# Keys and queries of batches 3 to 7 loaded by tokens and turned by DMA transposes, in a kernel for attention with beacons and an ELU layer

## The chip, the cores and the metric

The kernel runs on one core of one Trainium2 chip. The metric is the device time of one execution in microseconds (us); lower is better. A core has TensorE (PE, matrix products and transposes through a product with the identity), VectorE (DVE), ScalarE (ACT), GpSimd (POOL) and SyncE (SP), which here issues nearly all DMAs. TensorE writes to PSUM, from which VectorE or ScalarE copy. Each engine works through its own list of instructions in order, and waits on semaphores for the others.

## The reference

B = 8 batches, H = 8 heads, S = 576 tokens, 16 beacons for each batch and head, D = 64. Keys and values get the beacons ahead of the tokens; a token sees all beacons and the tokens up to itself. The attention's output, 4608 rows of 512, goes through two matrix products with an ELU between them (512 to 2048 to 512).

```python
    k_all = np.concatenate([beacon_k, k], axis=2)
    v_all = np.concatenate([beacon_v, v], axis=2)
    scores = scale * np.matmul(q, k_all.transpose(0, 1, 3, 2))
    causal[:, Nb:] = np.triu(np.ones((S, S), dtype=bool), k=1)
    scores = np.where(causal, -1000000000.0, scores)
    a = np.exp(scores - scores.max(-1, keepdims=True))
    a /= a.sum(-1, keepdims=True) + 1e-09
    attn_out = np.matmul(a, v_all)
    x = attn_out.transpose(0, 2, 1, 3).reshape(B * S, H * D)
    h = x @ w_in
    g = np.where(h > 0.0, h, np.exp(np.minimum(h, 0.0)) - 1.0)
    out = g @ w_out
```

All inputs lie in DRAM in fp32, and so does the output; the kernel computes with bf16 (scores) and fp16 (the rest).

## The kernel before

**The order.** The kernel is not written as loops. Each step is an `Op` with an engine, a key (its due time), an estimated duration, the steps that it depends on, and the buffer slots that it takes and gives back. `Plan.run` (L38) plays these through on a clock of its own: on each engine it starts the ready step with the lowest key whose slots are free, and then calls the steps' functions in the order found. So every engine's order of instructions, SP's too, comes from the keys and the estimated durations; the chip then runs each engine's list in order with semaphores. The steps of the pseudo-engine `DMA` stand for transfers; they issue nothing and only say when data are taken to have landed. One line of them is served by key, one after the other. `load` (L244) makes a step on SP and the transfer behind it, and L709 to L712 chain all loads in order of their keys. `place(b, a)` (L503) gives the key of batch b: 32 for each batch, 8 for each pair of heads, plus `SHIFT[b]`; `AT`, `AT0`, `PACES`, `W_AFTER`, `FIRST`, `LAG` and `URGE` (L490 to L501) are the other constants of the keys, and `ON_POOL` and `Q_ON_ACT` choose engines.

**Attention.** A unit of work is a pair of heads of one batch, n = 4 b + hp (32 pairs).

- `load_pair` (L263, DMA at L269): two DMAs load a pair's keys and queries, 288 KB each. A partition gets 9 neighbouring tokens of a head, so a run in DRAM is 9 x 64 fp32 values, 2304 B; keys lie on the even partitions, queries on the odd ones. `load_bk` (L255) and `cast_bk` (L260) bring a batch's beacon keys.
- `cast_pair` (L272): one instruction casts the pair to bf16 (tile `st`, 1152 values on each partition), on GpSimd for most pairs.
- `do_T` (L307; matmuls at L311 and L313): nine transposes of 128 x 128 on TensorE and one for the beacons, into a PSUM tile `tr` that shares its two slots (`sc`) with the scores. Batch 0 uses `do_T2` and `do_copy2` in place of `do_T`, `do_kT` and `do_qT`.
- `do_kT` (L343: two copies, L345 and L346) on VectorE and `do_qT` (L348: L351 on ScalarE or L353 on VectorE) copy `tr` into the bf16 tiles kT and qT, in order of tokens. There are `NKQ` = 4 such pairs of tiles.
- `do_SC` (L355): scores, keys on the partitions; `do_exp` (L368) exponentials on ScalarE into `et`; `do_mask` (L375) the causal mask on GpSimd.
- `load_v` (L285, DMA at L292) brings values by tokens, in 5 chunks of up to 128 tokens for each batch: a partition gets one token of all 8 heads, in runs of 64 fp32 values, 256 B. `cast_v` (L294) casts them on VectorE.
- `do_AV` (L383) multiplies with the values; a column of ones gives the sums. `do_norm` (L404: L411, L412) divides on VectorE into x16.
- x16 must be turned for the next product. Batches 0 and 1 do it on TensorE (`do_xT`, `do_xcopy`). From batch `XB` = 2 on `turn_x` (L280, L282) does it with five DMA transposes for a batch, issued by SP; each takes up to 128 rows of 512 fp16 values to 4 blocks of 128 partitions of `xT`.

**The ELU layer.** The 4608 rows are cut in 10 tiles (256, 256, then 512 rows). `do_mm1` (L444) makes a step of the hidden layer in PSUM (`hps`), `do_e` (L453) its exponential on ScalarE, `do_clamp` (L457) bounds it on GpSimd, `do_join` (L461) joins both on VectorE into `gt`; `do_mm2` (L471) multiplies with w_out into `ops`, `do_osb` (L480) copies on VectorE and `do_store` (L484) stores through SP. The weights come in four pieces each of w_in and w_out (512 KB each in fp16, 1 MB in DRAM), loaded and cast by DMAs that GpSimd issues (`load_w`, L298; `plan_w`, L545). Which step they come behind is `W_AFTER`: an index into `marks`, the sorted masks and beacon casts of the first batches.

PSUM's slots: `sc` 2, `ff` 4. Buffers in SBUF: `st` (fp32 pairs) 4, `sb` (bf16 pairs) 2, `vst` (fp32 values) 5, `gt` 20, `osb` 3.

Of the kernel before, what the change touches and what calls it, by code (L numbers as in the profile page):

```python
# [18 lines left out]
class Op:  # L19
    def __init__(self, eng, key, dur, fn, deps=(), take=(), give=(), mode=None, lat=0.03):  # L20
        self.eng, self.key, self.dur, self.fn = eng, key, dur, fn
        self.deps, self.take, self.give = [d for d in deps if d is not None], take, give
        self.mode, self.lat = mode, lat
        self.left, self.after = 0, []


class Plan:
# [10 lines left out]
    def run(self):  # L38
# [10 lines left out]
        mode = None  # L49
        for op in self.ops:  # L50
            if not op.left:
                heapq.heappush(ready[op.eng], (op.key, op.seq))
        events, order, now, n_left, tick = [], [], 0.0, len(self.ops), 0
        while n_left:
            for eng in ready:
                if free[eng] > now + 1e-9:
                    continue
# [36 lines left out]
            while events and events[0][0] <= now + 1e-9:  # L94
# [6 lines left out]
                for o in op.after:  # L101
                    o.left -= 1
                    if not o.left:
                        heapq.heappush(ready[o.eng], (o.key, o.seq))
# [8 lines left out]
def kernel(  # L113
# [86 lines left out]
    NG, NET, NKQ = 20, 8, 4  # L200
# [22 lines left out]
    kTs = [big.tile([P, SKP], BF16, name=f"kT_{i}") for i in range(NKQ)]  # L223
    qTs = [big.tile([P, S], BF16, name=f"qT_{i}") for i in range(NKQ)]
# [5 lines left out]
    with tc.tile_pool(name="psum", bufs=1, space=bass.MemoryType.PSUM) as psum:  # L230
# [4 lines left out]
            "st": 4, "sb": 2, "bk": 1, "vst": 5,  # L235
# [8 lines left out]
        def load(key, dur, fn, deps=(), take=(), issue=0.47):  # L244

            issue = add("SP", key, issue, fn, deps=deps, take=take)
            issues.append(issue)
            return add("DMA", key, dur, None, deps=[issue], lat=2.0)
# [6 lines left out]
        def load_bk(b):  # L255
            t = bks[b] = stage.tile([P, DM], FP32, tag="bk", name="bk32", bufs=1)
# [22 lines left out]

        def turn_x(b, blk):  # L280
# [4 lines left out]
        def load_v(b, jc):  # L285
            vst = vsts[b, jc] = stage.tile([P, H, D], FP32, tag="vst", name="vst", bufs=5)
# [197 lines left out]
        def do_store(tt, t4):  # L484
# [5 lines left out]
        SHIFT = [18.19, -1.67, -5.21, 9.28, 2.92, -5.56, -3.02, 18.21]  # L490
        AT = [-2.75, -0.54, -0.93, -0.06, 0.2, 1.01, 1.99, -16.61]
        AT0 = [[-45.78, -33.15, -38.79, -34.41], [-45.52, -23.75, -37.77, -41.96], [-33.6, -16.81, -31.44, -41.61]]
        PACES = [(-10.52, 1.48, 24.15, -2.31), (-10.42, 4.31, 27.52, 4.6), (37.71, 0.81, 11.65, 4.01), (83.94, 2.16, 31.7, 1.22), (112.53, 2.24, 29.18, 2.45)]
        W_AFTER = [[21.51, 12.09, 17.39, 6.76], [7.67, 24.47, 24.74, 25.24]]
        ON_POOL = "20010220"
        X_ON_ACT = "00"
        LAG = 17.55
        URGE = 72.32
        Q_ON_ACT = "01111110"
        FIRST = (  # L500
            "q2 k1 q1 v2 v1 k2 k3 q3 q5 v0 q4 k4 k5 v4 b1 v3 k6 q6 v6 v5 v9 q7 k7 v8 v7 ").split()  # L501
# [240 lines left out]
```

## Time and profile before

| | |
|---|---|
| median of 3 runs | 368.67 us (368.13 to 369.1) |
| the profiled execution's own time | 367.97 us |
| its span, from the first to the last instruction | 366.2 us |
| granted TensorE clock, mean | 0.989 |
| transposes of keys and queries on TensorE, L311 and L313, batches 1 to 7 | 280 matmuls in 28 groups |
| casts of pairs on GpSimd, L278 | 25, mean 1149 ns |
| copies to kT on VectorE, L345 and L346 | 28 each, mean 754 and 155 ns |
| copies to qT on ScalarE, L351 | 24, mean 649 ns |
| DMA transposes of x on SP, L282 | 30, median 1250 ns of issue, 2.5 us to landing |
| loads of keys and queries, L269 | 64, median 0.61 us of issue, 4.2 and 4.5 us to landing |
| loads of v, full chunks | 24, 5.3 us to landing |
| DMA queue of SP, share of 16 engines' span | 43.4% |
| DMA queue of GpSimd (weights) | 7.0% |

How to read it: the span lacks what lies around the first and last instruction. Busy time of an engine is the time in which one of its instructions ran; instructions of TensorE overlap each other. A row of 40 digits gives the busy share of 40 equal slices of the span, in tenths. The view of waits says which instruction waited for which other, for how long in total, how many times, and the longest. The DMA share of a stage is the mean over the core's 16 DMA engines of the time that packets took; two queues at work together can take it over 1.

### The profile page before, as it was taken

The page shows a single profiled execution, that of the slowest core. Times are in us where ns is not written, and L with a number is a line of the kernel's source. Part 1 is how long each engine was busy: PE and PEld are TensorE (multiplying, and loading weights), DVE is VectorE, ACT ScalarE, POOL GpSimd, SP SyncE. Part 2 cuts the span into 40 slices and gives each one's busy share as a digit, 9 for nine tenths or more (in the row PEclk, how much of TensorE's full clock was granted, in tenths as well). Part 3 has the DMA queues.
Part 4 walks back from the last instruction along what each step waited for, and adds up shares of the span by engine and source line. Part 5 has one row for each costly group of instructions (what it writes and reads, how often), then busy time and mean ns, then how long its engine had stood idle before and what let it go on. Part 6 is the DMA issues. An engine that isn't in the chain of part 4 may idle for free.

```text
span 366.2 us, 8353 instructions
## 1 busy us (share of the span) xinstructions
PE 346.9 (95%) x3240; PEld 191.7 (52%) x3240; DVE 213.3 (58%) x454; ACT 205.3 (56%) x308; POOL 190.6 (52%) x363
## 2 busy tenths in 40 slices
PE   1796999999999999999999999999999999999995
PEld 1564775755465556555555554544555544444442
DVE  1575367778864777765756765555666554554321
ACT  3775683568857786767677666435546534333100
POOL 3383582658855866757466656335534434344200
PEclk9998799999999999999999999999999999999999
DMA  7999995788137966957696600220000221000022
GB/s 215 295 235 243 235 164 148 179 233 285 55 68 203 273 83 161 208 146 197 143 235 170 135 30 29 57 68 29 31 29 30 57 68 57 30 29 29 30 94 78
DMA packets 73256, 46.54 MB, mean 127 GB/s; under 512 B 56321, under 2 KB 60417, under 8 KB 73217
## 3 DMA queue, kind: packets, MB, share of 16 engines
q1 hardware_dynamic: 68848, 41.53, 43.4%
q0 software_dynamic: 4224, 4.19, 7.0%
q8 instruction: 25, 0.41, 0.5%
q10 hardware_dynamic: 144, 0.29, 0.2%
q14 instruction: 15, 0.11, 0.1%
HBM read 37.22 MB, written 9.44 MB: 127 GB/s over the span
## 4 chain that ended last, share of the span: by engine, by line
PE 86%; DMA 5%; DVE 2%; POOL 2%; ACT 2%; SPq 1%; issue 1%; ACTq 0%; DVEq 0%
PE ops L476 34%; PE hps L449 33%; PE sc L362 7%; PE av L396 7%; PE tr L311 3%; DMA w_in<-in_moe_w_in_dram 3%; DMA st<-in_q_dram 1%; POOL et L377 1%; PE tr L321 1%; DMA vst<-in_v_dram 1%; ACT et L371 1%; DVE kT L345 1%; DVE gt L468 1%; SPq L282 0%; DVE v L296 0%
## 5 line engine op out<-in xcount | busy, mean ns | idle before, releaser
L449 PE MATMUL hps<-xT,w_in 128*128 128x512 f16 (+1 forms) x640 | 146.0, 363 | 2.8 <-DMA w_in<-in_moe_w_in_dram 2.2
L476 PE MATMUL ops<-w_out,gt 128*128 128x512 f16 x576 | 144.2, 379 | 0.0
L468 DVE SCALAR_TENSOR_TENSOR gt<-e,hps 128x512 f16<-128x512 f32 x144 | 97.6, 684 | 79.5 <-POOL e L459 79.3
L459 POOL TENSOR_SCALAR e<-e 128x512 f32<-128x512 f32 x144 | 89.5, 624 | 104.3 <-ACT e L455 101.5
L455 ACT ACTIVATE e<-hps 128x512 f32<-128x512 f32 x144 | 85.5, 599 | 90.8 <-PE hps L449 86.9
L371 ACT ACTIVATE et<-sc 128x800 f16<-128x800 f32 (+3 forms) x128 | 103.9, 864 | 22.0 <-PE sc L362 18.8
L449 PEld LDWEIGHTS <-w_in 128*128 128x128 f16 x640 | 60.5, 99 | 59.3 <-DMA w_in<-in_moe_w_in_dram 2.3
L476 PEld LDWEIGHTS <-gt 128*128 128x128 f16 x576 | 52.4, 98 | 57.5 <-issue 3.0
L377 POOL TENSOR_SCALAR_AFFINE_SELECT et<-et 128x256 f16<-128x256 f16 (+2 forms) x160 | 60.0, 402 | 40.4 <-ACT et L371 37.3
L396 PEld LDWEIGHTS <-et 128*128 128x128 f16 (+1 forms) x960 | 37.3, 100 | 10.8 <-issue 1.9
L396 PE MATMUL av<-v,et 128*128 128x65 f16 (+1 forms) x960 | 41.5, 197 | 0.6 <-POOL et L377 0.6
L362 PE MATMUL sc<-qT,kT 64*128 64x80 bf16 (+3 forms) x704 | 37.2, 238 | 3.4 <-ACT et L371 1.8
L482 DVE COPY osb<-ops 128x512 f32<-128x512 f32 x36 | 24.8, 689 | 23.8 <-PE ops L476 23.6
L362 PEld LDWEIGHTS <-kT 64*128 64x128 bf16 x704 | 21.8, 97 | 25.4 <-issue 19.2
L412 DVE TENSOR_TENSOR x<-av,rl 128x256 f16<-128x256 f32 (+2 forms) x68 | 32.0, 471 | 2.3
L278 POOL CAST st<-st 128x1152 bf16<-128x1152 f32 x25 | 28.7, 1149 | 8.1 <-PE tr L313 6.4
L351 ACT ACTIVATE qT<-tr 128x576 bf16<-128x576 bf16 x24 | 15.6, 649 | 19.8 <-DVE kT L346 12.0
L345 DVE COPY kT<-tr 128x576 bf16<-128x576 bf16 x28 | 21.1, 754 | 8.1 <-PE tr L313 7.7
L411 DVE RECIPROCAL rl<-av 128x4 f32<-128x4 f32 (+2 forms) x68 | 12.5, 183 | 16.6 <-PE av L396 15.5
L296 DVE CAST v<-vst 128x512 f16<-128x512 f32 (+1 forms) x40 | 18.9, 489 | 4.3 <-DMA vst<-in_v_dram 4.3
L311 PEld LDWEIGHTS <-st 128*128 128x128 bf16 x252 | 16.1, 98 | 5.6 <-issue 0.4
L311 PE MATMUL tr<-identb,st 128*128 128x128 bf16 x252 | 18.6, 219 | 0.1
(32 smaller groups left out, 69.0 us busy)
## 6 DMA issues: line engine op xcount, KB each, us to landing
st<-in_k_dram SPq DMA_DIRECT2D x32, 288.0 KB, 4.2
out_dram<-osb SPq DMA_DIRECT2D x36, 256.0 KB, 2.1
st<-in_q_dram SPq DMA_DIRECT2D x31, 288.0 KB, 4.5
vst<-in_v_dram SPq DMA_DIRECT2D x24, 256.0 KB, 5.3
w_in<-in_moe_w_in_dram POOLq DMA_DIRECT2D x4, 512.0 KB, 9.0
w_out<-in_moe_w_out_dram POOLq DMA_DIRECT2D x4, 512.0 KB, 8.4
vst<-in_v_dram SPq DMA_DIRECT2D x8, 224.0 KB, 4.0
vst<-in_v_dram SPq DMA_DIRECT2D x8, 160.0 KB, 5.0
```

Source lines behind the costliest of these rows:

```text
L278: eng.tensor_copy(out=dst, in_=src)
L311: nc.tensor.transpose(out=tr[:, P * g:P * g + P], in_=b16s[n][:, g].rearrange("p h d -> p (h d)"), identity=identb)
L362: nc.tensor.matmul(out=sc[:, h, o:o + w], lhsT=kT[D * h:D * h + D, P * jc:P * jc + P], rhs=qT[D * h:D * h + D, q0:q0 + w], start=True, sto ...
L371: nc.scalar.activation(out=et[:, :, 0:w], in_=scs[n, u][:, :, 0:w], func=AFT.Exp, bias=0.0, scale=float(1.0 / (D ** 0.5)))
L377: nc.gpsimd.affine_select(out=et[:, :, c0:c0 + dw], in_=et[:, :, c0:c0 + dw], compare_op=ALU.is_ge, fill=fill0, base=q0 + NB - P * jc, pat ...
L396: nc.tensor.matmul(out=av[:, c:c + D + 1], lhsT=ets[n, CUT.unit_of[jc, at]][0:m, h, col:col + P], rhs=v16[0:m, jc, 2 * hp + h, 0:D + 1], s ...
L412: nc.vector.tensor_tensor(out=x16s[b % 2][:, blks[0]:blks[0] + nb, P * hp:P * hp + P].rearrange("q i (h d) -> q i h d", d=D), in0=av[:, :, ...
L449: nc.tensor.matmul(out=hps[:, (hi - lo) * j:(hi - lo) * (j + 1)], lhsT=w_in16[:, cc, P * fc:P * fc + P], rhs=xT[cc][:, lo:hi], start=(cc = ...
L455: nc.scalar.activation(out=e, in_=hpss[tt, i], func=AFT.Exp, bias=0.0, scale=1.0)
L459: nc.gpsimd.tensor_scalar(out=e, in0=e, scalar1=1.0, scalar2=0.0, op0=ALU.min, op1=ALU.max)
L468: nc.vector.scalar_tensor_tensor(out=gt, in0=es[tt, i], scalar=1.0, in1=hpss[tt, i], op0=ALU.subtract, op1=ALU.max)
L476: nc.tensor.matmul(out=ops, lhsT=gts[tt, fc][:, P * t4:P * (t4 + 1)], rhs=w_out16[:, fc, :], start=(fc == 0), stop=(fc == NFC - 1))
```

## The change

From batch `PE_B` = 3 on, keys and queries take another way.

- They are loaded as v is (`load_tok`): for each batch 5 chunks of keys and 5 of queries, each up to 128 tokens of all 8 heads, in runs of 256 B. Beacon keys are the first 16 rows of the first key chunk, with a DMA of their own. Two chunks share an fp32 buffer.
- They are cast in 6 instructions for each batch (`cast_tok`): two chunks at once (1024 values on each partition), the fifth alone (512 values). The string `TOK` says which are on GpSimd ("1") and which on VectorE ("0").
- Each chunk is turned by one DMA transpose from SP (`turn_tok`) straight into kT or qT, 10 for each batch. It waits for the cast and for the scores of the batch two before.
- kT and qT are now two tiles for all four pairs of a batch (`kTa`, `qTa`), used by batches in turn: `NKQ` goes from 4 to 8 pairs. `gt` goes from 20 to 18 buffers, `vst` from 5 to 4, and beacon keys of the first batches use a `vst` buffer.
- The first scores of a batch from 3 on wait for all ten of its DMA transposes (`ready = turned[b]`). For these batches no transposes on TensorE and no copies to kT and qT are made, and no beacon casts.

Besides, the planner's picture of DMA changes: transfers are served in the order in which they were issued, on two lines (SP's and that of the weights) that take turns; at most 9 loads of SP are let into its line at once (`dq`); a piece of weights is four transfers. In the program itself the queues stay as they were: SP's for all but the weights (and one first load), GpSimd's for the weights. All constants of the keys were set anew, so the order of steps differs in all batches, with other engines for some casts of the first two batches (`ON_POOL`), copies to qT of batches 1 and 2 on VectorE (`Q_ON_ACT`), and other marks for the weights.

```diff
--- before.py
+++ after.py
...
 class Op:
-    def __init__(self, eng, key, dur, fn, deps=(), take=(), give=(), mode=None, lat=0.03):
+    def __init__(self, eng, key, dur, fn, deps=(), take=(), give=(), mode=None, lat=0.03, queue=0):
         self.eng, self.key, self.dur, self.fn = eng, key, dur, fn
         self.deps, self.take, self.give = [d for d in deps if d is not None], take, give
-        self.mode, self.lat = mode, lat
+        self.mode, self.lat, self.queue = mode, lat, queue
...
         free = dict.fromkeys(pending, 0.0)
-        mode = None
+        mode, lines, turn = None, ([], []), 0
+        def arrive(o):
+            if o.eng == "DMA":
+                lines[o.queue].append(o)
+            else:
+                heapq.heappush(ready[o.eng], (o.key, o.seq))
         for op in self.ops:
             if not op.left:
-                heapq.heappush(ready[op.eng], (op.key, op.seq))
+                arrive(op)
...
                 if free[eng] > now + 1e-9:
+                    continue
+                if eng == "DMA":
+                    if lines[0] or lines[1]:
+                        turn = 1 - turn if lines[1 - turn] else turn
+                        op = lines[turn].pop(0)
+                        free[eng] = now + op.dur
+                        heapq.heappush(events, (free[eng], tick, None))
+                        heapq.heappush(events, (free[eng] + op.lat, tick + 1, op))
+                        tick += 2
...
                 while first[eng] < len(line) and line[first[eng]][1] in done:
...
                     if not o.left:
-                        heapq.heappush(ready[o.eng], (o.key, o.seq))
+                        arrive(o)
...
         for _, _, op in order:
...
-    NG, NET, NKQ = 20, 8, 4
+    NG, NET, NKQ = 18, 8, 2 * HP
+    PE_B = 3
...
     stage = ctx.enter_context(tc.tile_pool(name="stage", bufs=2))
...
     x16s = [big.tile([P, NKC, DM], FP16, name=f"x16_{i}") for i in range(2)]
-    kTs = [big.tile([P, SKP], BF16, name=f"kT_{i}") for i in range(NKQ)]
-    qTs = [big.tile([P, S], BF16, name=f"qT_{i}") for i in range(NKQ)]
+    kTa = [big.tile([P, HP, SKP], BF16, name=f"kT_{i}") for i in range(2)]
+    qTa = [big.tile([P, HP, S], BF16, name=f"qT_{i}") for i in range(2)]
+    kTs = [t[:, hp] for t in kTa for hp in range(HP)]
+    qTs = [t[:, hp] for t in qTa for hp in range(HP)]
...
     bk16s = [big.tile([P, DM], BF16, name=f"bk16_{i}") for i in range(2)]
...
             "sc": 2, "ff": 4, "av": 2, "ops": 1, "et": NET, "rl": 2, "e": NE, "gt": NG, "osb": 3,
-            "st": 4, "sb": 2, "bk": 1, "vst": 5,
+            "st": 4, "sb": 2, "dq": 9, "vst": 4,
...
         add = plan.add
...
-            issue = add("SP", key, issue, fn, deps=deps, take=take)
+            issue = add("SP", key, issue, fn, deps=deps, take=take + ["dq"])
             issues.append(issue)
-            return add("DMA", key, dur, None, deps=[issue], lat=2.0)
+            return add("DMA", key, dur, None, deps=[issue], lat=2.0, give=["dq"])
...
         add("SP", -1e6, 0.8, None)
...
         def load_bk(b):
-            t = bks[b] = stage.tile([P, DM], FP32, tag="bk", name="bk32", bufs=1)
+            t = bks[b] = stage.tile([P, H, D], FP32, tag="vst", name="bk32", bufs=4).rearrange("p h d -> p (h d)")
...
+        def rows_of(is_k, c):
+            if not is_k:
+                return 0, min(P, S - P * c), P * c
+            r0 = NB if c == 0 else 0
+            return r0, kc_sz[c] - r0, P * c - NB + r0
+        def load_tok(b, is_k, c):
+            if (b, is_k, c // 2) not in f32s:
+                f32s[b, is_k, c // 2] = stage.tile([P, 2, G * D], FP32, tag="st", name="st32", bufs=4)
+            t = f32s[b, is_k, c // 2].rearrange("p h f -> p (h f)")[:, DM * (c % 2):DM * (c % 2) + DM]
+            t = t.rearrange("p (h d) -> p h d", h=H)
+            r0, n, lo = rows_of(is_k, c)
+            if is_k and c == 0:
+                nc.sync.dma_start(out=t[0:NB], in_=beacon_k[b].rearrange("h n d -> n h d"))
+            nc.sync.dma_start(out=t[r0:r0 + n], in_=(k if is_k else q)[b, :, lo:lo + n, :].rearrange("h s d -> s h d"))
+        def cast_tok(b, is_k, c, m, eng):
+            o = b16s[b, is_k, c // 2] = stage.tile([P, G, 2, D], BF16, tag="sb", name="st16", bufs=2)
+            r0, n, _ = rows_of(is_k, c + m - 1)
+            n = n if m == 1 else P
+            eng.tensor_copy(
+                out=o.rearrange("p g h d -> p (g h d)")[0:n, 0:DM * m],
+                in_=f32s[b, is_k, c // 2].rearrange("p h f -> p (h f)")[0:n, 0:DM * m])
+        def turn_tok(b, is_k, c):
+            r0, n, lo = rows_of(is_k, c)
+            t = (kTa if is_k else qTa)[b % 2]
+            nc.sync.dma_start_transpose(
+                out=t[:, :, P * c:P * c + r0 + n],
+                in_=b16s[b, is_k, c // 2].rearrange("p g h d -> p (g h d)")[0:r0 + n, DM * (c % 2):DM * (c % 2) + DM])
...
         def load_v(b, jc):
-            vst = vsts[b, jc] = stage.tile([P, H, D], FP32, tag="vst", name="vst", bufs=5)
+            vst = vsts[b, jc] = stage.tile([P, H, D], FP32, tag="vst", name="vst", bufs=4)
...
             r0 = NB if jc == 0 else 0
...
-        SHIFT = [18.19, -1.67, -5.21, 9.28, 2.92, -5.56, -3.02, 18.21]
-        AT = [-2.75, -0.54, -0.93, -0.06, 0.2, 1.01, 1.99, -16.61]
-        AT0 = [[-45.78, -33.15, -38.79, -34.41], [-45.52, -23.75, -37.77, -41.96], [-33.6, -16.81, -31.44, -41.61]]
-        PACES = [(-10.52, 1.48, 24.15, -2.31), (-10.42, 4.31, 27.52, 4.6), (37.71, 0.81, 11.65, 4.01), (83.94, 2.16, 31.7, 1.22), (112.53, 2.24, 29.18, 2.45)]
-        W_AFTER = [[21.51, 12.09, 17.39, 6.76], [7.67, 24.47, 24.74, 25.24]]
-        ON_POOL = "20010220"
+        SHIFT = [-1.59, -8.11, -4.8, -3.41, 4.52, 5.53, 8.01, 5.8]
+        AT = [-10.75, -2.37, -0.67, -1.23, -0.1, 1.04, 1.11, -20.16]
+        AT0 = [[-58.54, -53.13, -35.03, -42.4], [-45.14, -42.0, -36.41, -38.19], [-5.63, -27.76, -50.44, -20.85]]
+        PACES = [(-8.99, 2.27, 22.92, 3.9), (-2.72, 2.83, 27.52, 4.24), (38.17, 0.5, 9.24, 2.86), (79.65, 1.96, 26.14, 0.79), (105.01, 2.1, 30.59, 2.17)]
+        W_AFTER = [[7.88, -52.99, -9.09, 6.95], [16.42, 25.9, 20.56, 31.58]]
+        DMA_AT = [-127.66, -67.18, 46.75]
+        TOK = ("111001", "010110", "101011", "011001", "000000")
+        ON_POOL = "01202200"
         X_ON_ACT = "00"
-        LAG = 17.55
-        URGE = 72.32
-        Q_ON_ACT = "01111110"
+        LAG = 13.62
+        URGE = 62.52
+        Q_ON_ACT = "00011111"
         FIRST = (
-            "q2 k1 q1 v2 v1 k2 k3 q3 q5 v0 q4 k4 k5 v4 b1 v3 k6 q6 v6 v5 v9 q7 k7 v8 v7 ").split()
+            "v1 q1 k2 k1 k4 v0 q3 k3 v3 q2 v2 v4 q6 b1 q4 k7 q5 k5 v7 q7 v8 k6 v5 v6 v9 ").split()
...
             return 32 * (b - 1) + 8 * a + SHIFT[b]
...
             if hp == 0:
-                got = load(load_key(f"b{b}", place(b, 0) - 31), 0.2, partial(load_bk, b), take=["bk"])
+                got = load(load_key(f"b{b}", place(b, 0) - 31), 0.2, partial(load_bk, b), take=["vst"])
                 bk_in[b] = add("POOL", place(b, -0.9), 0.6, partial(cast_bk, b),
-                               deps=[got] + last_T.get(b - 2, []), give=["bk"])
+                               deps=[got] + last_T.get(b - 2, []), give=["vst"])
...
             gots = []
...
             got = add("POOL", after.key + 0.01, 0.8, partial(load_w, which, f4), deps=[after])
-            got = add("DMA", f4 - 300, 3.2, None, deps=[got], lat=2.5)
+            for _ in range(4):
+                got = add("DMA", 0, 0.8, None, deps=[got], lat=2.0 if _ == 3 else 0.0, queue=1)
             w_at.update({(which, 4 * f4 + c): got for c in range(4)})
+        turned, last_SC = {}, {}
+        def plan_tok(b):
+            turned[b] = []
+            for is_k in (True, False):
+                for c in range(0, NKC, 2):
+                    m = min(2, NKC - c)
+                    i = (0 if is_k else 0.5) + c // 2
+                    gots = [load(place(b, 0) - 30 + i + 0.01 * j, 1.2, partial(load_tok, b, is_k, c + j),
+                                 take=["st"] if j == 0 else [], issue=1.1 if is_k and c + j == 0 else 0.6) for j in range(m)]
+                    on_dve = TOK[b - PE_B][3 * (not is_k) + c // 2] == "0"
+                    cast = add("DVE" if on_dve else "POOL", place(b, DMA_AT[0]) + i, 0.36 * m if on_dve else 0.53 * m,
+                               partial(cast_tok, b, is_k, c, m, nc.vector if on_dve else nc.gpsimd),
+                               deps=gots, take=["sb"], give=["st"])
+                    for j in range(m):
+                        s = add("SP", place(b, DMA_AT[1]) + i, 1.25, partial(turn_tok, b, is_k, c + j),
+                                deps=[cast] + last_SC.get(b - 2, []))
+                        turned[b].append(add("DMA", place(b, DMA_AT[1]) + i, 0.6, None, deps=[s],
+                                             give=["sb"] if j == m - 1 else [], lat=1.9))
...
             b, hp = divmod(n, HP)
...
             key = AT0[0][hp] - 4 if b == 0 else at(AT[1])
-            ready = plan_T2(n, key) if b == 0 else plan_T(n, key)
+            ready = plan_T2(n, key) if b == 0 else plan_T(n, key) if b < PE_B else turned[b]
...
             steps = [((0,), AT0[0][hp]), ((1, 2), AT0[1][hp]), ((3,), AT0[2][hp])] if b == 0 else \
...
                 last_kq[n] = SC
+                last_SC.setdefault(b, []).append(SC)
...
                     w = CUT.width[u]
...
                             s = add("SP", at(AT[7]), 1.25, partial(turn_x, b, blk), deps=part.pop(blk))
-                            done = add("DMA", at(AT[7]), 0.5, None, deps=[s], lat=2.2)
+                            done = add("DMA", at(AT[7]), 0.6, None, deps=[s], lat=1.9)
...
                                 if lo <= BLOCKS[blk][0] < hi:
...
-        for t in kTs:
-            nc.vector.memset(t[:, SK:SKP], 0.0)
+        for t in kTa:
+            nc.vector.memset(t[:, :, SK:SKP], 0.0)
...
             plan_v(b)
+            if b >= PE_B:
+                plan_tok(b)
             for hp in range(HP):
-                plan_loads(b * HP + hp)
+                if b < PE_B:
+                    plan_loads(b * HP + hp)
...
```

## The prediction

> **What bounds the kernel now.** I read the shares of the engines first, then the same span in 40 slices, then who waited for whom on TensorE, and last the chain of waits in the middle of the span.
>
> ```profile
> span 366.2 us, 8353 instructions
> ...
> PE 346.9 (95%) x3240; PEld 191.7 (52%) x3240; DVE 213.3 (58%) x454; ACT 205.3 (56%) x308; POOL 190.6 (52%) x363
> ...
> PE   1796999999999999999999999999999999999995
> ...
> DMA  7999995788137966957696600220000221000022
> ```
>
> TensorE is busy 346.9 of 366.2 us, no other engine above 58%, and the row of slices puts TensorE's gaps in the first five slices and the last. The view of TensorE's waits from 50 us to the end has one entry:
>
> ```profile
> PE sc L362 <- ACT qT L351: 0.5, 1, 0.5
> ```
>
> So from 50 to 361 us nothing but TensorE's own work sets the time, and a TensorE instruction removed there shortens the kernel by its slot, as long as the other engines, the sync queue (SP) and the DMA engines keep up. The 19.3 us of gaps are 14.6 us in the first 50 us (start of loads, first pairs, the first weights) and the last copy and store.
>
> **What a removed transpose group is worth.** For batches 3 to 7, 20 pairs of heads lose their group of ten transposes. The chain of waits around one such group, in columns of start, length and what ran:
>
> ```profile
> 144.46 0.86 PE hps L449 x4
> 145.32 0.50 PE tr L311 x9
> 145.82 0.06 PE tr L313
> 145.88 0.18 PE av L396 x6
> ```
>
> From the first transpose to the next piece it is 145.88 - 145.32 = 0.56 us. The table of stages, restricted to that tile, gives the same group more:
>
> ```profile
> 200.00:210.00 10.00, 0.72 (x10) 0.82 (x2) 0.65 (x1) 1.00 0.69 170
> ```
>
> 0.72 us is the time from the first start to the modelled end of the last, and its last 0.16 us lie under the work behind. The start-to-start slot is what TensorE gets back: 20 x 0.56 = 11.2 us; the upper bound is 20 x 0.72 = 14.4 us. I take 11.2. The Trainium skill (Trainium Kernel Development and Optimization, Performance Expectations) says that matmul busy time is a bad measure because matmuls are pipelined. By that rule the 0.72 is not to be used, by the busy row alone the time would be 3.2 us lower; the trace agrees with the rule, 0.56 against 0.72.
>
> **What goes and comes on the other engines.** VectorE loses the copies to kT (754 + 155 ns, 20 times, 18.2 us) and batch 7's to qT (4 x 746 ns, 3.0); ScalarE loses 16 copies to qT (649 ns, 10.4 us); GpSimd loses 20 casts of pairs (1149 ns, 23.0) and 5 of the beacons (600 ns, 3.0). The casts by tokens come in: by the string TOK VectorE gets 12 of 1024 elements and 4 of 512, GpSimd 8 and 6. Scaled from the casts of 1152 elements (750 ns on VectorE, 1149 on GpSimd), that is 12 x 0.67 + 4 x 0.35 = 9.4 us and 8 x 1.02 + 6 x 0.55 = 11.5 us. So from batch 3 on VectorE has 11.8, ScalarE 10.4 and GpSimd 14.5 us less to do. Against that the new string for qT moves the copies of batches 1 and 2 from ScalarE to VectorE, 8 x 0.75 = 6 us in a stage (57 to 97 us) where VectorE is busy 31.0 of 40. All of this lies under TensorE, at a cost of nothing; without the cover a late copy costs the score step behind it.
>
> **The DMA engines.** This is what the change pays with. The tables of stages (length, busy time of PE, PEld, DVE, ACT and POOL, granted clock, DMA share, GB/s):
>
> ```profile
> 97.00:103.00 6.00, 6.00 (x74) 3.36 (x72) 4.38 (x10) 5.30 (x9) 4.67 (x9) 1.00 0.32 101
> 103.00:110.00 7.00, 7.00 (x82) 4.03 (x81) 4.08 (x10) 3.31 (x5) 3.68 (x7) 1.00 0.38 74
> ...
> 300.00:309.00 9.00, 9.00 (x44) 4.09 (x42) 4.68 (x8) 3.58 (x6) 3.58 (x6) 1.00 0.08 30
> ...
> 57.00:97.00 40.00, 39.88 (x489) 24.03 (x488) 31.03 (x73) 26.20 (x39) 25.40 (x47) 1.00 0.69 194
> 103.00:163.00 60.00, 59.49 (x666) 33.34 (x664) 39.45 (x86) 41.65 (x62) 39.98 (x74) 1.00 0.72 172
> 163.00:213.50 50.50, 50.50 (x551) 28.29 (x550) 32.52 (x73) 35.41 (x52) 30.89 (x60) 1.00 0.68 160
> ```
>
> Share times length is busy time of all 16 engines; sync's timeline tells what was issued. 97 to 103 holds two loads by pairs: 1.92 us, 0.96 each. 103 to 110 holds five DMA transposes of x and next to nothing else: 2.66, 0.53 each. 300 to 309 holds one store, 0.72. From 57 to 97 there are 14 loads by pairs, 4 stores and 10 chunks of v: 27.6 - 13.4 - 2.9 = 11.3, or 1.13 a chunk. A chunk of v comes in runs of 256 B, as the token loads of the change do. From 103 to 163: 16 pairs, 5 stores, 12 chunks, 10 transposes: 43.2 - 15.4 - 3.6 - 13.6 = 10.6, so a transpose beside loads takes 1.06; 163 to 213.5 gives 1.02 in the same way. A transpose thus has the bounds 0.53 and 1.06, and I take 1.04, the row with loads beside it.
>
> Added in batches 3 to 7: 50 token chunks at 1.13 for 40 pairs at 0.96 (+18.1), and 50 transposes (26.5 to 52): +45 to +70 on the 186 us (50.9%) of now. A batch then needs 10 x 1.13 + 5 x 1.13 (v) + 15 x 1.04 (k, q and x) + 4.5 x 0.72 (stores) = 35.8 us of the DMA engines, and TensorE works (346.9 - 11.2)/8 = 42.0 us for a batch: 85%. Now the DMA engines idle from 215 us on but for stores and two rounds of x, and the change may use that time: kT and qT are held for two whole batches, so a batch can be loaded, cast and turned while the one before it is computed. I cost the DMA at nothing, with that as the cover. The Trainium skill (DMA: Bandwidth & Descriptors, Latency and other measured facts) gives DMA transposes 261 GB/s; an estimate from it is 131 KB / 261 = 0.50 us, like the lone row (0.53) and not the loaded one (1.04). By it a batch would need 27.7 us, 66%.
>
> **Sync's queue.** Five transposes take 6.51 us of issue:
>
> ```profile
> 103.39 6.51 SPq L282 DMA_TRANSPOSE xT<-x  x5
> ```
>
> So 1.26 us each: 50 more are 63 us, 50 token issues at v's 0.55 and 5 of beacons are 30, 45 go (27). Now 63 x 0.61 + 48 x 0.46 + 8 x 0.5 + 36 x 0.4 + 30 x 1.26 = 116 us; then 182 of some 355. Behind a transpose that waits for its cast or for the scores two batches back stand stores (three output buffers) and the loads of v. Half of the queue's time is free; cost nothing, else as in the last rival.
>
> **New waits.** A cast on VectorE or GpSimd waits for its load, with joins, clamps and masks behind it. Of 40 casts of v four waited for the load, 4.3 us in all, 2.0 at most. 30 token casts at that frequency: 3.2 us, most of it slack of engines at 58%; below nothing is excluded, since waiting only takes time. Bounds 0 and 3.2, and I take 0.5: four waits of that kind now cost TensorE one gap of 0.5.
>
> **The head.** The first pair's cast goes from ScalarE (1157 ns) to VectorE (750): -0.4. The first projection waits 2.2 us for w_in, and two w_in pieces are now tied to the earliest marks, not to the 12th and 17th: up to -2.2. Both together take 2 x 1 MB / 248 GB/s (the rate of the first 36 us) = 8.5 us of DMA time that comes ahead of loads of batches 0 and 1: up to +8.5. The order of the first loads is new and shows no side. I take 0, nearer the low end, since the saved wait is on the chain and the pushed loads only partly.
>
> **Sum** against the profiled execution's own 367.97 us: -11.2 + 0.5 + 0 = -10.7, so 357.3; against the median of 368.67 it is 358.0. I forecast **357.8** us.
>
> **The rivals.**
> (a) **More than forecast.** The 0.72 is the true price (-3.2) and w_in's wait goes (-2.6 with the cast): 352. For it: the wait for w_in is on the chain. Against: the starts 0.56 apart.
> (b) **Half given back.** Either w_in pushes the first attention back, up to 8.5 us, or late loads hold VectorE and GpSimd in their queues: 3 waits of 2.0 us that reach TensorE. 357.8 + 6 = 364. For it: DMA share 1.08 in the first 36 us, two queues already overlapping. Against: the first three batches still load by pairs.
> (c) **No gain.** The new waits happen to equal 11 us, or TensorE's slots were held by something that the view doesn't show: 368.7.
> (d) **Slower: the DMA engines become the bound from batch 3 on.** Before 103 us they were busy 88 of 103 us, and batch 3 needs 11.3 + 10.4 - 7.7 = 14 us more by about then; from there each batch needs 35.8 us. The order on sync's queue, two buffers for the cast tokens and the wait of turns for the scores two batches back keep them from being used throughout. At a share of 0.78 a batch takes 45.9 us, 3.9 more than TensorE, in five batches 19.5: 377. It becomes slower once a batch lies 2.2 us over TensorE's 42.0, at a share under 0.81. For it: the longest stages of loads and transposes reached only 0.72. Against: these were not waited for, and TensorE has three batches of projections in store (some 3.4 tiles) when batch 3 is due.
>
> **How the numbers follow.** Chances: forecast (354 to 361) 0.45, (a) 0.08, (b) 0.19, (c) 0.04, (d) 0.24. The likeliest one's own range is 354 to 361. Low end: (a)'s 352. High end: 374, which takes in (b) whole, (c), and the near part of (d); outside lie 0.03 below and about 0.15 above. A difference under 0.3% (1.1 us) can't be told from none here. Faster: 0.45 + 0.08 + 0.19 = 0.72; same 0.04; slower 0.24.
>
> **What would show it.** TensorE busy at about 332 to 336 us and full from 50 us on; the transposes in groups of ten only before batch 3; VectorE and ScalarE some 10 us lower each; DMA busy 230 to 256 us, with loads and transposes reaching past 215 us; no waits for the score steps on the transposes' landing. The prediction is wrong if TensorE shows gaps of several us between 90 and 300 us before scores of batches 3 to 7 (d), before joins whose engine waited for a load, or a first projection much after 35.6 us (b).

## The result, and the profile after

| | median | ratio to the kernel before, 95% interval |
|---|---|---|
| before, in the same comparison | 368.4 us | |
| changed kernel | 378.89 us (377.52 to 379.34, 4 runs) | 1.0277 (1.0244 to 1.031) |

The change makes the kernel 2.8% slower. Ratios and intervals here and below are worked out over the executions in the faster of two states that a program shows, so they need not be the quotient of two medians. The head of the page of the changed kernel, its profiled execution (378.56 us), with the same rows as before:

```profile
span 376.9 us, 7895 instructions
...
PE 338.4 (90%) x3040; PEld 179.8 (48%) x3040; DVE 209.4 (56%) x432; ACT 192.3 (51%) x284; POOL 178.3 (47%) x352
...
PE   2587999999996896998969999689999999999995
...
DMA  7999999757885579998895998692201210100022
```

TensorE has 8.5 us less to do (346.9 to 338.4), but the span grew by 10.7, so its gaps grew from 19.3 to 38.5 us. They are no longer in the head alone: the row shows a 6, 8 and 6 in slices 13, 14 and 16 and more up to slice 27, all while batches 3 to 7 go through attention. Ten-microsecond stages give 19.4 us of gaps between 50 us and 260 us, against 0.6 before. Two stages (columns as in the tables of the prediction):

```profile
110.00:150.00 40.00, 31.25 (x262) 14.78 (x259) 17.02 (x35) 18.83 (x28) 16.68 (x33) 0.91 0.70 147
190.00:200.00 10.00, 6.55 (x47) 2.59 (x46) 3.16 (x7) 3.12 (x5) 2.95 (x6) 0.83 0.55 92
```

In both, every engine is less busy than usual and the DMA share is 0.70 and 0.55: neither a compute engine nor the 16 DMA engines are full. What TensorE waited for from 50 us on (the four longest entries), and VectorE's waits for values, before (L296) and after (L347):

```profile
PE hps L500 <- DVE gt L519: 6.6, 4, 3.2
PE hps L500 <- issue: 3.6, 1, 3.6
PE hps L500 <- DMA xT<-x: 3.4, 1, 3.4
PE hps L500 <- DVE x L463: 2.8, 2, 1.4
```

```profile
DVE v L296 <- DMA vst<-in_v_dram: 4.3, 4, 2.0
DVE v L347 <- DMA vst<-in_v_dram: 16.8, 10, 3.9
```

TensorE waits for joins and norms of VectorE, once for x to be turned, and once, from 116 us on, for nothing that the profile names ("issue"). VectorE itself had stood 16.8 us (4.3 before) at casts of v whose load had not landed. The chain of waits across one of the three longest gaps (3.2 us from 141 us on) leads one step further back:

```profile
135.69 0.57 DVE x L463
136.26 0.54 SPq L327
...
136.85 1.26 SPq L333
...
138.16 4.94 DMA vst<-in_v_dram
...
143.12 0.43 DVE v L347
143.55 0.61 DVE gt L519
...
144.20 3.37 PE hps L500 x8
```

Two loads of v were issued at 138.16, behind a DMA transpose of keys or queries (L327) and one of x (L333) in SP's line; they landed 4.94 us later; the cast and the join behind them came late and TensorE stood for 3.24 us. SP's own timeline (start, length, line, what, how many) shows how full that line is:

```profile
129.43 0.41 SPq L343 DMA_DIRECT2D vst<-in_v_dram  x1
129.94 0.50 SPq L537 DMA_DIRECT2D out_dram<-osb  x1
130.49 1.23 SPq L343 DMA_DIRECT2D vst<-in_v_dram  x2
131.81 2.41 SPq L333 DMA_TRANSPOSE xT<-x  x1
134.32 1.19 SPq L327 DMA_TRANSPOSE kT<-st  x1
135.60 1.20 SPq L327 DMA_TRANSPOSE qT<-st  x1
136.85 1.26 SPq L333 DMA_TRANSPOSE xT<-x  x1
138.16 2.28 SPq L343 DMA_DIRECT2D vst<-in_v_dram  x2
```

One issue follows the other with hardly 0.1 us between them. Adding up the lengths of such rows, SP is occupied during 0.96 of the time from 100 to 200 us and 0.95 of that from 200 to 250; before it was 0.67 and 0.30. This number, called SP's share below, is worked out in this way for each run. (A row of several issues holds the short pauses between them; without these it is 0.94 and 0.93. Where a row holds a long pause, as before from 200 us on, its single issues are counted.)

SP's share is not all plain issue. If no issue is counted with more than the median of its line, the stretch from 100 to 200 us adds up to 0.76 (0.55 before). The rest are issues that took longer, such as the 2.41 us above for a transpose of usually 1.25; the traces don't tell whether these waited for a step or were held by the DMA queue.

### The profile page after: what moved, and what is told of

Its sections match the earlier page's. It is cut to its first block, busy times and chain, and to the rows that moved or that the text cites. A ratio compares the mean times of both kernels' runs of the same rounds, so it can differ in the third digit from the quotient of the medians.

```text
span 376.9 us, 7895 instructions
## 1 busy us (share of the span) xinstructions
PE 338.4 (90%) x3040; PEld 179.8 (48%) x3040; DVE 209.4 (56%) x432; ACT 192.3 (51%) x284; POOL 178.3 (47%) x352
## 4 chain that ended last, share of the span: by engine, by line
PE 74%; DMA 11%; DVE 4%; POOL 3%; issue 3%; ACT 2%; SPq 2%; DVEq 0%; POOLq 0%; ACTq 0%
PE ops L527 31%; PE hps L500 29%; PE av L447 6%; PE sc L413 6%; DMA vst<-in_v_dram 6%; DMA kT<-st 2%; DMA qT<-st 2%; DMA bk<-in_beacon_k_dram 1%; PE tr L362 1%; POOL e L510 1%; POOL et L428 1%; PE tr L372 1%; ACT et L422 1%; DVE x L463 1%; DVE st L320 1%
## 5 line engine op out<-in xcount | busy, mean ns | idle before, releaser
L500 PE MATMUL hps<-xT,w_in 128*128 128x512 f16 (+1 forms) x640 | 147.5, 366 | 16.5 <-DVE gt L519 6.6
L422 ACT ACTIVATE et<-sc 128x736 f16<-128x736 f32 (+3 forms) x128 | 104.0, 864 | 33.1 <-PE sc L413 29.6
L428 POOL TENSOR_SCALAR_AFFINE_SELECT et<-et 128x256 f16<-128x256 f16 (+2 forms) x160 | 60.8, 406 | 45.6 <-ACT et L422 44.5
L463 DVE TENSOR_TENSOR x<-av,rl 128x384 f16<-128x384 f32 (+2 forms) x68 | 32.1, 471 | 2.3
L347 DVE CAST v<-vst 128x512 f16<-128x512 f32 (+1 forms) x40 | 19.6, 501 | 16.9 <-DMA vst<-in_v_dram 16.8
L462 DVE RECIPROCAL rl<-av 128x6 f32<-128x6 f32 (+2 forms) x68 | 12.4, 182 | 16.7 <-PE av L447 16.4
L320 DVE CAST st<-st 128x1024 bf16<-128x1024 f32 (+2 forms) x16 | 11.2, 706 | 15.6 <-DMA qT<-st 6.1
L320 POOL CAST st<-st 128x1024 bf16<-128x1024 f32 (+2 forms) x14 | 12.4, 884 | 14.8 <-DVE rl L462 4.8
L372 PE MATMUL tr<-identb,st 128*128 128x128 bf16 x36 | 4.6, 311 | 9.0 <-DVE st L297 6.1
L372 PEld LDWEIGHTS <-st 128*128 128x128 bf16 x36 | 3.5, 142 | 10.0 <-DVE st L297 6.1
L385 ACT ACTIVATE qT<-tr 128x256 bf16<-128x256 bf16 (+1 forms) x8 | 3.1, 452 | 9.0 <-PE tr L375 9.0
```

Of the source, the lines that this page charges most:

```text
L320: eng.tensor_copy(out=o.rearrange("p g h d -> p (g h d)")[0:n, 0:DM * m], in_=f32s[b, is_k, c // 2].rearrange("p h f -> p (h f)")[0:n, 0:D ...
L422: nc.scalar.activation(out=et[:, :, 0:w], in_=scs[n, u][:, :, 0:w], func=AFT.Exp, bias=0.0, scale=float(1.0 / (D ** 0.5)))
L428: nc.gpsimd.affine_select(out=et[:, :, c0:c0 + dw], in_=et[:, :, c0:c0 + dw], compare_op=ALU.is_ge, fill=fill0, base=q0 + NB - P * jc, pat ...
L463: nc.vector.tensor_tensor(out=x16s[b % 2][:, blks[0]:blks[0] + nb, P * hp:P * hp + P].rearrange("q i (h d) -> q i h d", d=D), in0=av[:, :, ...
L500: nc.tensor.matmul(out=hps[:, (hi - lo) * j:(hi - lo) * (j + 1)], lhsT=w_in16[:, cc, P * fc:P * fc + P], rhs=xT[cc][:, lo:hi], start=(cc = ...
```

## The experiments

All times are medians of a comparison, each on one chip, with the kernel before, which lay between 366.6 and 368.4 us; ratios are to it. Where the order is said to stay, the planner's order is exactly that of the changed kernel and only what a step issues differs.

**No transposes at all.**

```diff
         def turn_tok(b, is_k, c):
             r0, n, lo = rows_of(is_k, c)
             t = (kTa if is_k else qTa)[b % 2]
-            nc.sync.dma_start_transpose(
...
+            return
```

> The order of all steps as in the changed kernel, but the 50 DMA transposes of keys and queries are not issued (batches 3 to 7 compute with the keys and queries left in the tiles by batches 1 and 2). Theory A (the transposes of the change, by the time they hold the DMA engines and SP, make values, x and casts late): TensorE's gaps after 50 us, 18.9 us, all but go, 359 to 364 us. Theory B (the token loads in runs of 256 B fill the DMA engines): the gaps stay for the larger part, 371 to 377. Theory C (the new order itself, whatever DMA does): 374 to 379.

354.01 us, ratio 0.9643 (0.9606 to 0.968), below the range of theory A. The span and TensorE's only wait from 50 us on:

```profile
span 351.9 us, 7796 instructions
```

```profile
PE hps L498 <- DVE gt L517: 0.5, 1, 0.5
```

With the transposes gone, the token loads, their casts and the whole new order run without a gap. So theories B and C in their plain form fall: neither the loads alone nor the order costs anything. SP's share from 100 to 200 us is 0.69.

**Transposes of 16 rows.**

```diff
             nc.sync.dma_start_transpose(
-                out=t[:, :, P * c:P * c + r0 + n],
-                in_=b16s[b, is_k, c // 2].rearrange("p g h d -> p (g h d)")[0:r0 + n, DM * (c % 2):DM * (c % 2) + DM])
+                out=t[:, :, P * c:P * c + 16],
+                in_=b16s[b, is_k, c // 2].rearrange("p g h d -> p (g h d)")[0:16, DM * (c % 2):DM * (c % 2) + DM])
```

> Each of the 50 transposes turns 16 rows in place of up to 128; the rest of kT and qT keeps what batches 1 and 2 left. SP still issues 50 transposes, at the same places of its line. Theory A1 (the time that a transpose holds the DMA engines is what hurts): 359 to 365 us. Theory A2 (SP's issue, 1.25 us each, with what waits behind in its line, is what hurts): 374 to 379, if the issue still takes some 1.2 us; should the issue become short as well, the run tells less.

374.95 us, 1.0211 (1.0145 to 1.0277): 0.6% better than the changed kernel by the ratios, with intervals that overlap, where A1 expected some 4%. The lines of the transposes in this run (shortest, median, longest issue in ns) and of SP's DMA queue:

```profile
L327 SPq DMA_TRANSPOSE kT<-st x25: 1123/1163/2011, 74.1 to 245.2; - x25
L327 SPq DMA_TRANSPOSE qT<-st x25: 1112/1210/2041, 80.7 to 246.6; - x25
```

```profile
q1 hardware_dynamic: 112368, 42.36, 48.7%
```

A transpose of 16 rows takes SP as long to issue (1.16 and 1.21 us) as one of up to 128 (1.22). What the transposes move is nearly gone: the DMA engines are busy 210 us instead of 245 (the shares of all queues, 56.4% and 65.1%, times the spans), 35 us less, and at most 3.9 us come of it. So the transposes don't hurt by their traffic. What is left is their place in SP's line: their issue, or what SP waits for at them. SP's share stays 0.96, which leaves both open; the dummy loads below settle it.

**Token loads in long runs.**

```diff
-            nc.sync.dma_start(out=t[r0:r0 + n], in_=(k if is_k else q)[b, :, lo:lo + n, :].rearrange("h s d -> s h d"))
+            nc.sync.dma_start(
+                out=t[r0:r0 + n].rearrange("p h d -> p (h d)"),
+                in_=(k if is_k else q)[b].rearrange("h s d -> (h s) d")[H * lo:H * (lo + n)].rearrange("(p g) d -> p (g d)", g=H))
```

> The token loads of batches 3 to 7 read as many bytes, but in runs of 2048 B (other rows than the reference's, so the scores are of mixed tokens). Theory B (short runs): DMA busy falls from 245 us by 10 to 20 and most gaps go, 362 to 368 us. Theory A: the transposes stay, 374 to 379, at most 3 us gained.

360.34 us, 0.9825 (0.9779 to 0.9872), better than either theory expected and faster than the kernel before. The lines of the token loads in the changed kernel and in this run:

```profile
L314 SPq DMA_DIRECT2D st<-in_k_dram x25: 422/573/2104, 58.6 to 237.0; - x25
L314 SPq DMA_DIRECT2D st<-in_q_dram x25: 368/665/3112, 61.0 to 237.5; - x25
```

```profile
L314 SPq DMA_DIRECT2D st<-in_k_dram x25: 323/429/1837, 59.2 to 220.7; - x25
L314 SPq DMA_DIRECT2D st<-in_q_dram x25: 328/435/1872, 60.2 to 221.1; - x25
```

The issue of a load in short runs is longer, 0.57 and 0.67 us in the median against 0.43 and 0.44, 9 us over the 50; with the long ones among them the 50 issues add up to 42.0 us against 26.5, 15.5 less. DMA busy falls by 13 us, to 232 (64.3% of 360.8). SP's share from 200 to 250 us falls from 0.95 to 0.79; from 100 to 200 us it is still 0.94, so a share near 1 over some stretch is not yet a loss. The run changes issue and transfer together, so it doesn't say how its 18.5 us divide; after the run before, 13 us of DMA time alone are not the likelier part.

**Three cast buffers.** `bufs=2` to `bufs=3` for the cast tokens, `bufs=NG` to `bufs=17` for `gt`.

> Three buffers in place of two for the cast tokens (and 17 in place of 18 for gt to make room); the order stays. Theory D (casts on VectorE and GpSimd wait for a buffer that a transpose still reads, and hold up what is behind them): the waits of casts for transposes (17.7 us on the two engines) go, 366 to 371 us. Theories A and B: the transposes and values are as late as before, 375 to 379.

378.84 us, 1.0312 (1.026 to 1.0365). The waits of VectorE's token casts for transposes are gone, its waits for v from 50 us on grew from 13.4 to 19.9 us, and no time was gained. Theory D falls: a wait removed behind a full queue comes back at the next thing in that queue.

**Other issuers for part of SP's line.** `nc.sync` to `nc.scalar` in `load_tok`, in `load_v` and in `do_store`, one at a time; later `nc.sync` to `nc.gpsimd` in `load_tok`.

> The order stays; only the 55 token loads of keys, queries and beacons of batches 3 to 7 are issued by ScalarE in place of SP, so SP's line has some 45 us less between 57 and 240 us and the DMA engines the same work. Theory E (SP's line is the bound: occupied 95% of the time from 100 to 250 us, with transposes at 1.2 us of issue each whatever their size): the occupancy falls to some 0.75 and most of TensorE's 18.9 us of gaps go, 357 to 366 us. Theory F (the 16 DMA engines, or the landing times, are the bound): 373 to 380. ScalarE's own issue and waits may cost up to 5 us in either.

> As the run before, but the 48 loads of v and of beacon values are the ones that ScalarE issues; tokens stay with SP. Theory E: 25 us less on SP, and v no longer stands behind transposes, 360 to 369 us. Theory F: 373 to 380.

> Only the 36 stores are issued by ScalarE, each behind its wait for VectorE's copy. Theory E: SP loses about 15 us of issue, but those between 100 and 250 us are only 14 stores with 8 us, so 367 to 374. Theory F: 375 to 381. ScalarE waits for VectorE's copies at the end of each block of rows, which may cost a few us.

> The changed kernel's order, with the 55 token loads issued by GpSimd (some 0.8 us each by the weights' rows) in place of SP. ScalarE was held up to 5 us by two such issues in the run where it issued them. Theory E, if GpSimd isn't held up like that: SP's occupancy falls as in that run (0.73) and the time to 358 to 368. If GpSimd's masks and clamps now come late behind the issues and their waits for buffers: 370 to 380.

| | time, us | ratio, 95% interval | SP's share, 100 to 200 us |
|---|---|---|---|
| tokens from ScalarE | 373.55 | 1.0166 (1.0108 to 1.0225) | 0.74 |
| values from ScalarE | 384.84 | 1.046 (1.0403 to 1.0517) | 0.87 |
| stores from ScalarE | 372.92 | 1.0128 (1.0077 to 1.0179) | 0.96 |
| tokens from GpSimd | 367.19 | 0.9998 (0.9975 to 1.0021) | 0.78 |

The run with stores came within theory E's range. Those with tokens and values from ScalarE missed what theory E gave for them, and the one with tokens lies in the range of theory F. SP's share fell, but a part of the line only moved. ScalarE's timeline in the run with tokens:

```profile
103.02 5.30 ACTq L314 DMA_DIRECT2D st<-in_q_dram  x2
108.43 0.60 ACT L506 ACTIVATE e<-hps 128x512 f32<-128x512 f32 x1 [5.41 <-DMA st<-in_k_dram]
```

Two issues held ScalarE for 5.30 us while an exponential of the hidden layer waited behind them for 5.41; TensorE's waits for ScalarE and what follows it replaced those for values. With the values it begins in the head: 32.2 us of TensorE work in the first 50 us instead of 34.8. GpSimd takes 0.92 us for such an issue (1.14 at most), and there the loss of the change is gone: from 378.9 to 367.2, within theory E's range though at its upper end. TensorE's gaps from 50 to 260 us fall from 19.4 to 9.6 us, not to none. With another issuer these loads also go through another DMA queue (ScalarE's then holds the DMA engines for 18.0% of the span, GpSimd's 21.9% in place of 7.0), so these runs alone don't tell SP's issue from SP's queue.

**SP's line filled with issues that do nothing.** To the kernel without transposes, in place of each:

```diff
+            for _ in range(2):
+                s = scratch[len(used) % 8]
+                used.append(0)
+                nc.sync.dma_start(out=s, in_=moe_w_in[0:16, 0:16])
```

> The kernel without the 50 transposes (354.0 us), with two loads of 1 KB that nothing waits for in place of each, 100 in all at some 0.5 us of issue. They give SP's line back about what the transposes took, without the transposes' traffic and without their waits for casts. Theory E, by occupancy alone: 362 to 376. If what hurts is that SP waits at a transpose for its cast, or what the transposes do to other transfers: 354 to 358.

> The kernel without the 50 transposes, with one load of 1 KB that nothing waits for in place of each (some 25 us of issue on SP, half of the run with two). Theory E as a threshold: SP's line has room for that (two thirds to three quarters occupied from 100 to 200 us without them), so 354 to 358 us. If issue on SP cost the same from the first us on, half of the 11.2 us of the run with two: 359 to 361.

> Three in place of each, some 75 us of issue on SP. Theory E: the line was full with two (0.96 from 100 to 200 us), so the 25 us more come out nearly whole, 380 to 394 us. If the loss with two came from single badly placed loads and not from a full line: 367 to 375.

| dummy loads for each transpose | time, us | ratio, 95% interval | SP's share, 100 to 200 us |
|---|---|---|---|
| 0 | 354.01 | 0.9643 (0.9606 to 0.968) | 0.69 |
| 1 | 355.5 | 0.9683 (0.9634 to 0.9733) | 0.89 |
| 2 | 365.22 | 0.9847 (0.9799 to 0.9895) | 0.96 |
| 3 | 385.33 | 1.0494 (1.0422 to 1.0566) | 0.96 |

By the medians the first 50 loads cost 1.5 us, the next 9.7, the last 20; by the ratios it is 1.5, 6 and 24. (The five executions with two dummies lie between 362.1 and 368.8 us, so the middle steps are known to a few us only.) The issues of the 50, 100 and 150 dummies add up to 29.5, 53 and 75 us:

```profile
L330 SPq DMA_DIRECT2D scratch<-in_moe_w_in_dram x150: 407/418/1648, 76.7 to 258.0; - x150
```

No step waits for them and they wait for no cast. They move so little that the DMA engines are busy 209 to 212 us in all four runs. Yet the same gaps appear: with three, TensorE's gaps from 50 to 260 us are 20.3 us (19.4 in the changed kernel), and VectorE waits 22.7 us for v from 50 us on. SP's line has free room for the first 50; the second 50 cost a part of their 24 us of issue, the last 50, with the line full, about the whole of theirs (21 us). The 50 transposes add up to 68 us of issue in the changed kernel and 65 with 16 rows. On the straight line between two and three dummies that would be 379 and 376 us, and 378.9 and 375.0 were measured; so close a fit is partly luck, given the spread with two.

This shows theory E: what lies in SP's line ahead of the loads makes the loss, whatever it moves. Another limit of the line, on transfers under way, can be left out: SP's DMAs use eight semaphores in turn, and in the changed kernel from 50 us on the transfer before had landed at least 1.4 us before its semaphore was used again.

**From batch 5 on.** `PE_B = 5`, a dearer transpose in the planner, 0.06 us more for each step on SP, and all constants of the keys new:

```diff
-        self.eng, self.key, self.dur, self.fn = eng, key, dur, fn
+        self.eng, self.key, self.dur, self.fn = eng, key, dur + (0.06 if eng == "SP" else 0.0), fn
...
-    PE_B = 3
+    PE_B = 5
...
-                        turned[b].append(add("DMA", place(b, DMA_AT[1]) + i, 0.6, None, deps=[s],
-                                             give=["sb"] if j == m - 1 else [], lat=1.9))
+                        turned[b].append(add("DMA", place(b, DMA_AT[1]) + i, 1.04, None, deps=[s],
+                                             give=["sb"] if j == m - 1 else [], lat=2.0))
```

> Only batches 5 to 7 go by tokens and DMA transposes (30 in place of 50), and the order is planned again with a dearer transpose (1.04 us in the DMA line and 2.0 to land, in place of 0.6 and 1.9) and 0.06 us more for each issue on SP, all keys chosen anew. TensorE loses 12 groups, 6.7 us. Theory E: with 20 transposes and 16 net loads fewer, and so planned, SP's line stays under some 0.9 in every stretch of 50 us and few gaps come after 50 us: 361 to 366 us, faster than both kernels. If the new way costs by its mere use, whatever SP's load: 368 to 374.

363.01 us over 6 runs, 0.9887 (0.9846 to 0.9927): faster than both kernels. TensorE's waits from 50 us on, whole:

```profile
PE hps L500 <- DVE gt L519: 1.9, 1, 1.9
PE tr L362 <- POOL e L510: 0.4, 1, 0.4
```

SP's share is 0.71 from 100 to 150, 0.94 from 150 to 200 and 0.89 from 200 to 250: the expected 0.9 was passed in one stretch without harm. Batches, prices and keys changed together here; the run agrees with theory E and doesn't show which of the three did it.

## Why the prediction was wrong

- **What bounds the kernel, and what a group is worth: right.** Without the transposes of the change the kernel runs at 354.0 us, 13.7 below its partner before. 11.2 were forecast for the groups. TensorE's busy time fell by 14.5 (346.9 to 332.4), which would fit 0.72 us a group, the bound that the forecast laid aside; but a part of it is the clock. Before, TensorE ran from 30 to 40 us at a granted clock of 0.71 (row below), in this run the mean clock of the span is 1.00. By that row the clock is worth some 3 us (10 x 0.29, an estimate). By the 38 executions of the kernel before beside the experiments it is less: the six with a mean clock of 0.999 or 1.00 have a median of 366.4 us, the others 367.7. If nothing else differs, the groups are worth 10.8 to 12.4 us, 0.54 to 0.62 each.

```profile
30.00:40.00 10.00, 7.30 (x77) 5.18 (x77) 3.37 (x13) 4.38 (x6) 3.86 (x9) 0.71 1.21 239
```

- **The head:** taken as 0, with a range from -2.6 to +8.5. In the first 50 us TensorE is busy as long as before (34.8 and 35.3 us) at a clock of 1.00 in place of 0.93, so the head gained the 1 to 3 us of the clock. No run isolates it.
- **The other engines: right.** VectorE, ScalarE and GpSimd have 4, 13 and 12 us less, and none became the bound.
- **The DMA engines: right in size and in cost.** 45 to 70 us more were forecast, 58 were measured (187 to 245). Their traffic costs little: 35 us less of it gave at most 3.9 us. Rival (d) gave 377 us and the right batches, but named these engines as the full resource, and put the deciding point at a share of theirs under 0.81. From 100 to 250 us they were at 0.84, which by its own sum is 42.6 us a batch and no loss against the kernel before, and with transposes of 16 rows at 0.67 with nearly the same time. That its number came out is luck.
- **Sync's queue: this step failed.** "Half of the queue's time is free; cost nothing" set 182 us of issue against the whole span of 355. The price of one transpose was right in the median (1.26 forecast, 1.22 measured). But what was added lies almost whole between 57 and 250 us, beside the loads and x transposes that were there already, and from 100 us on the line is 0.96 full there. A mean over the span hid a full stretch, although the timeline of before had it: 0.67 from 100 to 200 us, 0.16 from 250 to 300. The 66 us net that were added are 13 a batch, and 2.4 batches fall into 100 us at 42 us each: 67 + 2.4 x 13 = 98 of 100 us, with the prediction's own prices for what is added. The sum was too small as well. All issues of SP add up to 149 us before and 236 in the changed kernel, against 116 and 182 in the prediction, which left out the long issues: the loads of v took 0.55 us in the median and 0.77 in the mean and were priced at 0.46. Token loads took 0.57 and 0.67 in the median, up to 3.1 us, in place of the 0.55 that was used.
- **New waits: mis-sized as a consequence.** At most 3.2 us were allowed, from the waits for v before. VectorE's waits for v alone are 16.8 us, because v stands in SP's line behind the new transposes.

The Trainium skill (DMA: Bandwidth & Descriptors, Issuing engines are not separate DMA queues) says that issuing from several engines saves only the sequencer's time, usually small beside the transfer. For one load that is so here: 0.57 and 0.67 us of issue, 4.6 and 4.8 us to landing for a full chunk. For the sum of a line it is not: token loads issued by GpSimd in place of SP, with the DMA engines busy as long (248 and 245 us), gave 11.7 us.

## What to carry to other kernels

Cost a queue that issues DMAs like an engine: count every issue with its measured length, stretch by stretch where the new ones will fall, and not over the span. Here, from a share of 0.69 to one of 0.89 over 100 us, added issues cost next to nothing; once the line was full (0.96), they cost about their own length on the critical path, through loads that have nothing to do with the change. A stretch of 50 us at 0.94 did no harm in the run from batch 5 on. Take the sum of the issues and not their median: the long ones count. To see whether traffic or issue hurts, shrink what each DMA moves and keep their number, or add DMAs that move next to nothing.

## What the runs showed of the hardware

- A DMA transpose from SP takes 1.16 to 1.21 us to issue with 16 rows and 1.22 with up to 128 (medians).
- A load of the same bytes takes longer to issue in runs of 256 B than in runs of 2048 B: 0.57 and 0.67 against 0.43 and 0.44 us (medians of the token loads). A load of 1 KB took 0.42.
- The issue of a token load can hold its engine: ScalarE 5.30 us for two, SP up to 3.1 for one. GpSimd's issues of the same loads took 0.70 to 1.14 us throughout. What the long ones waited for is not shown.
- In the changed kernel each of the three longest gaps on TensorE (3.2 to 3.6 us) comes with a granted clock of 0.83 in its own ten microseconds or the next (120 to 130, 140 to 150 and 190 to 200 us).
